# A position-bias layer computed from one constant tile of shifted log distances, half on ScalarE and half on VectorE

## The chip, the cores and the metric

The kernel runs on one core of a Trainium2 chip. The metric is the device time of one execution in microseconds (us). The kernel before was timed three times: 1243.59 us median, 1242.97 to 1249.49. A profile shows one further execution. TensorE is written PE, VectorE DVE, ScalarE ACT; SP is the queue from which all DMAs are issued.

## The reference

Attention with a learned position bias, then two gated feed-forward layers, all in fp32. The sizes are 4 batches, 8 heads, 576 positions, 64 columns per head, a hidden layer of 32 for the bias, 512 model columns, 1536 and 2048 gate columns, 2304 tokens.

```python
rel = (pos[:, None] - pos[None, :])
x = log1p(abs(rel)) / log1p(maximum(pos[:, None], 1.0))     # 576 x 576
h = maximum(x[..., None] @ w1 + b1, 0.0)                    # 32 hidden units
bias = h @ w2                                               # 8 heads
scores = q @ k.T / 8 + bias;  attn = softmax(scores);  o = attn @ v
x = (sigmoid(o @ w_gate) * (o @ w_val)) @ w_out             # first layer
h = x @ w_in;  out = (h * clip(h + 3, 0, 6) / 6) @ w_out2   # second layer
```

The numerator of x depends only on the distance between two positions, the denominator only on the row.

## The kernel before

The 576 query positions are cut into five chunks (QC): four of 128 and one of 64. For each chunk the kernel computes the bias of its rows, runs attention for its 16 units (a unit is a pair of heads of one batch; the last chunk has 8 units), and then runs the 68 weight steps of the two feed-forward layers on the chunk's 512 tokens (256 in the last).

**The bias.** Rows are taken in groups G of 16, eight groups to a chunk. The hidden layer of a group is a tile z of 128 partitions by 4 by 576: the 32 hidden units times 4 rows stand on the partitions, and the four slots g hold four rows each. Eight matmuls with w2b_t (`bias_out`, L157) turn it into 16 rows by 8 heads in PSUM; one eviction (L163 on ACT for chunk 1, L165 on DVE for the others) multiplies by 8 and a DMA stores the result to a DRAM tile, from which attention reads it per pair of heads (`bias_read`, L181).

For chunk 0 (the *lead*) x comes in as eight tiles of 288 KB (xt, L424). Matmuls with wz_t (`lead_hidden`, L121) spread x over the partitions with the weight w1 in it, ACT (L125) and DVE (L126) each take half of the result out of PSUM with bias and relu, and `lead_out` (L139) makes the output in two halves, one evicted on ACT (L144), one on DVE (L146). In the lead the order on PE, ACT, DVE and SP is the order of the program. Chunk 0's bias is stored before its first attention unit begins; two weight splits stand between.

For the other chunks x is loaded already spread over the partitions: `bias_load` (L107) brings 1152 KB per group, each row of x read 32 times, and ACT computes the relu in place in two halves of 1152 columns (L111). The tile z has three buffers.

**Attention.** `att_qk` (L212) makes scores, L227 on DVE adds the bias and takes the maximum as a minimum of negated scores, L237 on ACT the exponential, L247 on DVE the normalisation, L260 transposes on PE, L263 copies on ACT, L279 multiplies by v, and L295 and L296 split the result into two parts.

**The weights.** In the first pass over the steps (block 0) a weight tile arrives packed (L306) and `w_split` takes it apart with L321 and L331 on ACT and L322, L323, L326 and L332 on DVE; the result is also stored to DRAM (L333). Later blocks load it from there (L310). Each step is twelve matmuls (L348), and each step's evictions run on ACT and DVE (L357 and L359 make the two parts of a gate's result).

**The order of the work.** After the lead only PE's order is written by hand. Block k runs the 68 steps of chunk k; events with a due step are put between them: the bias of chunk k+1 in blocks 0 and 1 from step 2 on, one group per 1.5 steps, its matmuls in pairs of groups; the bias of chunk 3 in block 1 from step 22, one group per 5.2 steps; the bias of chunk 4 in block 2; and attention of chunk k+1 from step 21 on (from step 0.5 in blocks 2 and 3). On ACT, DVE and SP a planner orders the instructions by its own simulated times; each of these queues then runs in that order. Loads after the lead are held until the loads of the lead's last unit have been issued (`issue_after`).

Of the kernel before, what the change touches and what calls it, by code (L numbers as in the profile page):

```python
# [56 lines left out]
def fused_kernel(ctx: ExitStack, tc: tile.TileContext, qd, kd, vd, xp, xr, wz, zc, w2b, iden, wpack, out):  # L57
# [55 lines left out]
    def lead_hidden(G, j, xt):  # L113

        if j == 0:
            z_q[G] = z_p.tile([128, 4, S], F32, name="z")
        z = z_q[G]
        cs = slice(NI * j, NI * j + NI)
        ps = [s_ps(), s_ps()]
        for q in range(4):  # L120
            nc.tensor.matmul(  # L121
                out=ps[q // 2][:, q % 2, 0:NI], lhsT=wz_t[32 * q:32 * q + 32], rhs=xt[32 * q:32 * q + 32, G, cs],
                start=True, stop=True, tile_position=(32 * q, 0),
            )
        nc.scalar.activation(out=z[:, 0:2, cs], in_=ps[0][:, :, 0:NI], func=AF.Relu, bias=b1c)  # L125
        nc.vector.tensor_scalar(  # L126
            out=z[:, 2:4, cs], in0=ps[1][:, :, 0:NI], scalar1=b1c, scalar2=0.0, op0=ALU.add, op1=ALU.max
        )

    def lead_out(G, j):  # L130

        z = z_q[G]
        if j == 0:
            bo_q[G] = bo_p.tile([128, S], F32, name="bo")
        bo = bo_q[G]
        po = mm_ps()[:, 0:NI]
        cs = slice(NI * j, NI * j + NI)
        for g in range(4):
            nc.tensor.matmul(  # L139
                out=po[32 * g:32 * g + 32], lhsT=w2b_t, rhs=z[:, g, cs], start=True, stop=True,  # L140
                tile_position=(0, 32 * g),
            )
        if j == 0:
            nc.scalar.activation(out=bo[:, cs], in_=po, func=AF.Copy, scale=D ** 0.5)  # L144
        else:
            nc.vector.tensor_scalar(out=bo[:, cs], in0=po, scalar1=D ** 0.5, scalar2=None, op0=ALU.mult)  # L146
            nc.sync.dma_start(out=biasD[0][16 * G:16 * G + 16].rearrange("i h j -> (i h) j"), in_=bo)
# [390 lines left out]
def _positions():  # L538

    pos = np.arange(S)  # L540
    rel = (pos[:, None] - pos[None, :]).astype(np.float32)
    x = np.log1p(np.abs(rel)) / np.log1p(np.maximum(pos[:, None].astype(np.float32), 1.0))
    x = x.astype(np.float32)
    n = QC[0][1]
# [63 lines left out]
```

## Time and profile before

| | us |
|---|---|
| median of three runs | 1243.59 |
| profiled execution | 1242.72 |
| its span | 1240.9 |
| PE busy | 1188.8 |
| PE weight loads busy | 933.4 |
| DVE busy | 588.3 |
| ACT busy | 571.6 |
| moved by DMA | 332.43 MB |

The span is the time from the first to the last instruction of the profiled execution. A matmul in fp32 shows as two records. An engine's idle time is put down to what ended it; an engine runs its own instructions in order, so an instruction that waits holds those behind it. The clock column is the share of full speed that was granted to TensorE.

### The profile page before, as it was taken

What the parts mean: (1) busy time and instruction counts of PE and PEld (TensorE: products, weight loads), DVE (VectorE), ACT (ScalarE), POOL (GpSimd) and SP (SyncE); (2) the same over time, 40 slices, a digit from 0 to 9 for tenths busy, and PEclk for the clock granted to TensorE, in tenths of its full rate; (3) what the DMA queues carried; (4) which work ended last, traced back from release to release, by engine and by line L of the source; (5) the groups of instructions that cost most, each with busy time, mean ns of one, the idle gap of its engine ahead of it and who ended that gap; (6) DMA issues with size and microseconds to landing.
All of it is one profiled execution on the core that took longest, in us unless ns stands there. A gap on an engine that the chain in (4) does not pass through costs nothing.

```text
span 1240.9 us, 20018 instructions
## 1 busy us (share of the span) xinstructions
PE 1188.8 (96%) x7672; PEld 933.4 (75%) x7672; DVE 588.3 (47%) x1284; ACT 571.6 (46%) x1121; POOL 0.2 (0%) x4
## 2 busy tenths in 40 slices
PE   7797997999999999999999999999999999999998
PEld 3576665777778777677777777777778888788998
DVE  4786756899893333344343333253423323341232
ACT  4588775677672463455543333253412223341231
POOL 0000000000000000000000000000000000000000
PEclk9798988999999999999999999999999999999999
DMA  6779997999987896875878575767677676657997
GB/s 231 248 249 366 346 418 282 351 358 320 356 292 246 313 404 209 279 254 189 278 231 295 183 256 182 218 190 216 192 218 244 226 234 210 204 185 227 372 366 279
DMA packets 120160, 332.43 MB, mean 268 GB/s; under 512 B 20993, under 2 KB 35585, under 8 KB 116481
## 3 DMA queue, kind: packets, MB, share of 16 engines
q1 hardware_dynamic: 120064, 331.16, 78.0%
q8 instruction: 61, 1.00, 0.3%
q14 instruction: 35, 0.28, 0.1%
HBM read 280.12 MB, written 50.99 MB: 267 GB/s over the span
## 4 chain that ended last, share of the span: by engine, by line
PE 78%; DMA 8%; DVE 7%; ACT 4%; issue 2%; SPq 0%; ACTq 0%; DVEq 0%
PE ps L348 59%; PE ps L279 6%; DMA z<-xp 5%; PE ps L212 5%; PE ps L260 5%; PE ps L157 2%; DMA wd<-wpack 2%; ACT z L111 2%; PE ps L121 1%; DVE cm L323 1%; DVE wp L332 1%; DVE cm L326 1%; DVE s L227 1%; ACT s L237 1%; PE ps L139 1%
## 5 line engine op out<-in xcount | busy, mean ns | idle before, releaser
L348 PE MATMUL ps<-xyh,wp 128*128 128x512 f32 (+1 forms) x1600 | 483.8, 377 | 8.8 <-ACT pT L263 3.5
L348 PE MATMUL ps<-gh,wp 128*128 128x512 f32 (+1 forms) x1120 | 346.2, 380 | 2.8 <-DVE wp L332 1.5
L348 PEld LDWEIGHTS ps<-xyh,wp 128*128 128x128 f32 x1600 | 291.9, 190 | 73.8 <-issue 11.7
L348 PE MATMUL ps<-xyl,wp 128*128 128x512 f32 (+1 forms) x800 | 296.5, 371 | 0.7 <-DVE xyl L361 0.7
L348 PEld LDWEIGHTS ps<-gh,wp 128*128 128x128 f32 x1120 | 204.1, 189 | 46.7 <-issue 8.6
L348 PE MATMUL ps<-gl,wp 128*128 128x512 f32 (+1 forms) x560 | 207.1, 370 | 0.0
L348 PEld LDWEIGHTS ps<-xyl,wp 128*128 128x128 f32 x800 | 152.1, 190 | 23.7 <-DVE xyl L361 1.1
L263 ACT ACTIVATE pT<-ps 128x384 f32<-128x384 f32 x216 | 100.8, 487 | 116.8 <-PE ps L260 116.4
L237 ACT ACTIVATE s<-s,m 128x576 f32<-128x576 f32 x144 | 110.6, 771 | 67.1 <-DVE m L227 66.5
L357 ACT ACTIVATE gh<-tmp 128x512 fp32r<-128x512 f32 (+1 forms) x140 | 82.3, 588 | 113.0 <-DVE tmp L379 80.9
L359 DVE TENSOR_TENSOR gl<-tmp,gh 128x512 fp32r<-128x512 f32 (+1 forms) x140 | 89.3, 638 | 69.4 <-ACT gh L357 68.9
L227 DVE CUSTOM_DVE_ANT_0 s<-ps,bm 128x576 f32<-128x576 f32 x144 | 103.9, 753 | 30.0 <-PE ps L212 29.5
L348 PEld LDWEIGHTS ps<-gl,wp 128*128 128x128 f32 x560 | 106.3, 190 | 15.0
L260 PE MATMUL ps<-id_t,s 128*128 128x128 f32 x648 | 104.0, 280 | 9.9 <-DVE s L247 8.1
L260 PEld LDWEIGHTS ps<-id_t,s 128*128 128x128 f32 x648 | 80.1, 142 | 42.9 <-issue 13.2
L279 PE MATMUL ps<-pT,vt 128*64 128x128 f32 (+1 forms) x1600 | 98.3, 271 | 5.0 <-DVE xyl L296 4.4
L212 PE MATMUL ps<-kt,qt 64*128 64x288 f32 (+1 forms) x640 | 93.7, 435 | 8.0 <-DVE m L227 8.0
L279 PEld LDWEIGHTS ps<-pT,vt 128*64 128x64 f32 x1600 | 81.0, 139 | 24.8 <-issue 15.4
L379 DVE SCALAR_TENSOR_TENSOR tmp<-tmp,ps 128x512 f32<-128x512 f32 (+1 forms) x60 | 38.0, 633 | 126.4 <-PE ps L348 116.3
L111 ACT ACTIVATE z<-z,zc_t 128x1152 f32<-128x1152 f32 x56 | 72.5, 1342 | 23.8 <-DMA z<-xp 23.7
L385 DVE SCALAR_TENSOR_TENSOR tmp<-tmp,ps 128x512 f32<-128x512 f32 (+1 forms) x80 | 50.5, 631 | 66.9 <-ACT tmp L384 65.5
L296 DVE TENSOR_TENSOR xyl<-ps,xyh 128x128 fp32r<-128x128 f32 x72 | 20.8, 289 | 125.0 <-ACT xyh L295 125.0
(36 smaller groups left out, 727.8 us busy)
## 6 DMA issues: line engine op xcount, KB each, us to landing
wp<-wsp SPq DMA_DIRECT2D x272, 512.0 KB, 4.1
wd<-wpack SPq DMA_DIRECT2D x68, 512.0 KB, 5.9
wsp<-wp SPq DMA_DIRECT2D x68, 512.0 KB, 5.5
z<-xp SPq DMA_DIRECT2D x28, 1152.0 KB, 10.1
vt<-vd SPq DMA_DIRECT2D x80, 320.0 KB, 4.3
kt<-kd SPq DMA_DIRECT2D x80, 288.0 KB, 4.6
biasD<-bo SPq DMA_DIRECT2D x36, 288.0 KB, 8.4
bm<-biasD SPq DMA_DIRECT2D x16, 576.0 KB, 5.8
```

Of the source, the lines that this page charges most:

```text
L111: nc.scalar.activation(out=z, in_=z, func=AF.Relu, scale=w1c, bias=b1c)
L212: nc.tensor.matmul(out=ps[h][n * a:n * a + n, j, 0:NI], lhsT=qt[r, b + a, 0:n], rhs=kt[r, NI * j:NI * j + NI], start=True, stop=True, tile ...
L227: nc.vector.tensor_tensor_reduce(out=d["s"][:, h].rearrange("p (a j) -> p a j", a=2), in0=ps[h][:, :, 0:NI], in1=bm[:, h].rearrange("p (a ...
L237: nc.scalar.activation(out=s[:, h], in_=s[:, h], func=AF.Exp, scale=-1.0, bias=d["m"][:, h:h + 1], accum_out=r[:, h:h + 1],)
L260: nc.tensor.transpose(out=ps[:, t * NQ:t * NQ + NQ], in_=p[:, 128 * k:128 * k + 128], identity=id_t)
L263: nc.scalar.activation(out=d["pt"][:, 3 * part:3 * part + 3], in_=ps[:, 0:3 * NQ].rearrange("p (t n) -> p t n", t=3), func=AF.Copy,)
L279: nc.tensor.matmul(out=po[64 * h:64 * h + 64, n * a:n * a + n], lhsT=vt[:, v], rhs=pt[:, k, n * a:n * a + n], start=(t == 0), stop=(t == 4 ...
L348: nc.tensor.matmul(out=ps[:, 0:nt], lhsT=w[:, c, :], rhs=x[:, 0:nt], start=(first and c == 0 and i == 0), stop=(last and c == 3 and i == 2),)
L357: nc.scalar.activation(out=hi[:, 0:nt], in_=src, func=AF.Copy, scale=scale)
L359: nc.vector.tensor_tensor(out=lo[:, 0:nt], in0=src, in1=hi[:, 0:nt].bitcast(F32), op=ALU.subtract)
L379: nc.vector.scalar_tensor_tensor(out=th, in0=th, scalar=1.0, in1=ps, op0=ALU.add, op1=ALU.mult)
L385: nc.vector.scalar_tensor_tensor(out=t, in0=t, scalar=6.0, in1=ps, op0=ALU.min, op1=ALU.mult)
```

## The change

x is no longer loaded. One constant tile tz_t holds, on partition p, the numerators log1p(|distance|) for all distances, shifted by p mod 4 (1148 columns). The x of four rows is a window of 576 columns of it, at a place that depends on the rows; the reciprocal of the denominator times w1 is a scalar per partition in sc_t, one column for every four rows. For slots 0 and 1 ACT computes relu(s x + b). For slots 2 and 3 DVE computes max(s x, -b), which is smaller by b; the product of the missing b with w2, times 8, is a scalar per partition cv_t that the eviction adds. Four small DVE instructions and two small matmuls set up these scalars.

The lead uses the same functions as the other chunks: the loads of xt, the matmuls with wz_t and the evictions in halves are gone, and so are the loads into z. The upper part of tz_t is loaded first (700 of 1148 columns), the rest behind the loads of the first three units. z has two buffers in place of three. `bias_out` is cut into `bias_mm` (matmuls) and `bias_out` (eviction and store); after the lead, both groups' matmuls of a pair are issued before both evictions. The evictions use Identity with a bias in place of Copy on ACT, and a multiply and add on DVE.

```diff
-    z_p = pool("z", 3)
+    z_p = pool("z", 2)
...
+    nc.sync.dma_start(out=zc_t[:, 0:2], in_=zc)
+    nc.sync.dma_start(out=sc_t, in_=rd)
+    nc.sync.dma_start(out=tz_t[:, t0:], in_=tz[:, t0:])
     nc.sync.dma_start(out=w2b_t, in_=w2b)
+    nc.vector.tensor_scalar(out=sc_t, in0=sc_t, scalar1=zc_t[:, 0:1], scalar2=None, op0=ALU.mult)
+    nc.vector.tensor_scalar(out=zc_t[:, 2:3], in0=b1c, scalar1=-1.0, scalar2=None, op0=ALU.mult)
+    nc.vector.memset(cv_t, 0.0)
+    ps = mm_ps()
+    for g in (2, 3):
+        nc.tensor.matmul(
+            out=ps[32 * g:32 * g + 32, 0:2], lhsT=w2b_t, rhs=zc_t[:, 0:2], start=True, stop=True,
+            tile_position=(0, 32 * g),
+        )
+    nc.vector.tensor_scalar(out=cv_t[64:128], in0=ps[64:128, 1:2], scalar1=D ** 0.5, scalar2=None, op0=ALU.mult)
...
-    def bias_load(G):
-        z = z_q[G] = z_p.tile([128, 4, S], F32, name="z")
-        nc.sync.dma_start(out=z.rearrange("p g j -> p (g j)"), in_=xp[G:G + 1].broadcast_to([32, 4, 4 * S]))
-    def bias_hidden(G, g0, g1):
-        z = z_q[G][:, g0:g1]
-        nc.scalar.activation(out=z, in_=z, func=AF.Relu, scale=w1c, bias=b1c)
+    def bias_hidden(G, g):
+        if g == 0:
+            z_q[G] = z_p.tile([128, 4, S], F32, name="z")
+        t = 4 * G + g
+        z, x = z_q[G][:, g], tz_t[:, S - 4 - 4 * t:2 * S - 4 - 4 * t]
+        if g < 2:
+            nc.scalar.activation(out=z, in_=x, func=AF.Relu, scale=sc_t[:, t:t + 1], bias=b1c)
+        else:
+            nc.vector.tensor_scalar(
+                out=z, in0=x, scalar1=sc_t[:, t:t + 1], scalar2=zc_t[:, 2:3], op0=ALU.mult, op1=ALU.max
+            )
...
-            nc.scalar.activation(out=bv, in_=ps[:, :, 0:NI], func=AF.Copy, scale=D ** 0.5)
+            nc.scalar.activation(out=bv, in_=ps[:, :, 0:NI], func=AF.Identity, scale=D ** 0.5, bias=cv_t)
         else:
-            nc.vector.tensor_scalar(out=bv, in0=ps[:, :, 0:NI], scalar1=D ** 0.5, scalar2=None, op0=ALU.mult)
+            nc.vector.tensor_scalar(
+                out=bv, in0=ps[:, :, 0:NI], scalar1=D ** 0.5, scalar2=cv_t, op0=ALU.mult, op1=ALU.add
+            )
...
-        for G in range(NG0):
-            nc.sync.dma_start(out=xt[:, G], in_=xr[G])
         nc.sync.dma_start(out=id_t, in_=iden)
         for n in range(2):
             w_load(n)
         for u in us[0:3]:
             att_load(u, False)
-        for G in range(NG0 + 1):
-            for j in range(2):
-                if G < NG0:
-                    lead_hidden(G, j, xt)
-                if G:
-                    lead_out(G - 1, j)
+        nc.sync.dma_start(out=tz_t[:, 0:t0], in_=tz[:, 0:t0])
+        for G in range(QC[0][1] // 16 + 1):
+            if G < QC[0][1] // 16:
+                for g in range(4):
+                    bias_hidden(G, g)
+                bias_mm(G)
+            if G:
+                bias_out(G - 1)
...
-        ev = [(t0 - 3.0 + dt * min(g, 1), lambda G=G0 + g: bias_load(G)) for g in range(min(nG, 2))]
+        ev = []
         for g in range(nG):
-            def hidden(G=G0 + g, more=g + 2 < nG):
-                bias_hidden(G, 0, 2)
-                bias_hidden(G, 2, 4)
-                if more:
-                    bias_load(G + 2)
-            ev.append((t0 + dt * g, hidden))
+            ev.append((t0 + dt * g, lambda G=G0 + g: [bias_hidden(G, t) for t in range(4)]))
         for g in range(0, nG, 2):
             def outs(G=G0 + g):
+                for i in range(2):
+                    bias_mm(G + i)
                 for i in range(2):
                     bias_out(G + i)
```

## Rows read from the trace of the kernel before

**Rows 1.** The page: busy time, and TensorE's granted clock in 40 slices.

```profile
PE 1188.8 (96%) x7672; PEld 933.4 (75%) x7672; DVE 588.3 (47%) x1284; ACT 571.6 (46%) x1121; POOL 0.2 (0%) x4
...
PEclk9798988999999999999999999999999999999999
```

**Rows 2.** Windows: from:to, length, PE, PEld, DVE, ACT, POOL busy, clock, DMA share, GB/s.

```profile
84.70:116.40 31.70, 24.17 (x218) 18.82 (x216) 23.52 (x62) 28.99 (x61) 0.00 (x0) 0.84 0.96 363
...
131.30:171.90 40.60, 36.59 (x238) 24.72 (x237) 23.97 (x42) 30.54 (x43) 0.00 (x0) 0.92 1.01 395
...
189.90:218.00 28.10, 20.95 (x81) 15.05 (x82) 21.19 (x44) 15.83 (x28) 0.00 (x0) 0.88 0.73 264
218.00:365.00 147.00, 142.14 (x888) 110.29 (x888) 137.65 (x297) 104.50 (x217) 0.00 (x0) 1.00 0.96 344
...
500.00:568.00 68.00, 61.83 (x405) 46.56 (x404) 28.18 (x66) 35.23 (x66) 0.00 (x0) 0.97 0.76 260
568.00:672.00 104.00, 102.48 (x676) 79.20 (x675) 40.14 (x98) 49.17 (x97) 0.00 (x0) 1.00 0.78 255
```

**Rows 3.** Timeline of the first 44 us: start, length, engine, instruction, idle before.

```profile
2.11 3.76 SPq L424 DMA_DIRECT2D xt<-xr  x8
...
5.30 1.34 PE L121 MATMUL ps<-xt,wz_t 32*128 32x288 f32 x8 [5.30 <-DMA xt<-xr]
...
11.12 1.19 PE L139 MATMUL ps<-z,w2b_t 128*32 128x288 f32 x8
...
15.70 0.69 PE L139 MATMUL ps<-z,w2b_t 128*32 128x288 f32 x8
...
36.26 0.46 DVE L146 TENSOR_SCALAR bo<-ps 128x288 f32<-128x288 f32 x1 [0.49 <-ACT bo L144]
...
43.59 0.76 DVE L227 CUSTOM_DVE_ANT_0 s<-ps,bm 128x576 f32<-128x576 f32 x1 [0.38 <-DMA bm<-biasD]
```

**Rows 4.** Lines by shape: instruction, count | busy us, mean ns | idle before.

```profile
L111 ACT ACTIVATE z<-z,zc_t 128x1152 f32<-128x1152 f32 x56 | 72.5, 1342 | 23.8 <-DMA z<-xp 23.7
...
L357 ACT ACTIVATE gh<-tmp 128x512 fp32r<-128x512 f32 x112 | 70.6, 630 | 86.9 <-DVE tmp L379 62.6 <-DVE tmp L385 23.8
L247 DVE TENSOR_SCALAR s<-s,r 128x576 f32<-128x576 f32 x144 | 68.3, 516 | 2.0
...
L165 DVE TENSOR_SCALAR bo<-ps 128x576 f32<-128x576 f32 x20 | 15.0, 754 | 9.7 <-PE ps L157 9.7
L126 DVE TENSOR_SCALAR z<-ps,zc_t 128x576 f32<-128x576 f32 x16 | 13.1, 818 | 19.8 <-PE ps L121 17.0 <-issue 2.8
...
L125 ACT ACTIVATE z<-ps,zc_t 128x576 f32<-128x576 f32 x16 | 11.8, 740 | 14.4 <-PE ps L121 14.4
...
L357 ACT ACTIVATE gh<-tmp 128x256 fp32r<-128x256 f32 x28 | 11.7, 417 | 26.1 <-DVE tmp L379 18.3 <-DVE tmp L385 7.9
...
L125 ACT ACT_TABLE_LOAD x1 | 1.3, 1283 | 3.0 <-DMA zc_t<-zc 3.0
```

**Rows 5.** Timeline of ACT around L111, and PE's waits from 500 to 570.

```profile
94.44 2.59 ACT L111 ACTIVATE z<-z,zc_t 128x1152 f32<-128x1152 f32 x2 [0.50 <-DMA z<-xp]
...
106.05 2.61 ACT L111 ACTIVATE z<-z,zc_t 128x1152 f32<-128x1152 f32 x2
...
189.82 2.58 ACT L111 ACTIVATE z<-z,zc_t 128x1152 f32<-128x1152 f32 x2
...
193.06 0.66 ACT L321 ACTIVATE cm<-wd 128x512 f32<-128x512 f32 x1
...
505.39 2.59 ACT L111 ACTIVATE z<-z,zc_t 128x1152 f32<-128x1152 f32 x2 [4.40 <-DMA z<-xp]
...
L348 PE MATMUL ps<-xyh,wp 128*128 128x512 f32 x63 | 22.6, 423 | 3.5 <-ACT pT L263 3.5
```

**Rows 6.** DMA issues: KB each and median us to landing.

```profile
z<-xp SPq DMA_DIRECT2D x28, 1152.0 KB, 10.1
...
xt<-xr SPq DMA_DIRECT2D x8, 288.0 KB, 5.4
```

More of the change, by code (lines that the diff above doesn't have):

```diff
@@ L24 @@
 NF1, NF2 = DFF1 // 128, DFF2 // 128
-NG = S // 16
 QC = ((0, 128), (128, 128), (256, 128), (384, 128), (512, 64))
@@ L56, in fused_kernel @@
 @with_exitstack
-def fused_kernel(ctx: ExitStack, tc: tile.TileContext, qd, kd, vd, xp, xr, wz, zc, w2b, iden, wpack, out):
+def fused_kernel(ctx: ExitStack, tc: tile.TileContext, qd, kd, vd, tz, rd, zc, w2b, iden, wpack, out):
     nc = tc.nc
@@ L89, in fused_kernel @@
     wsp = dr_p.tile([NSTEP, 128, 2, 512], F32, name="wsp")
-    wz_t = const.tile([128, 128], F32, name="wz_t")
-    zc_t = const.tile([128, 2], F32, name="zc_t")
+    tz_t = const.tile([128, 2 * S - 4], F32, name="tz_t")
+    sc_t = const.tile([128, S // 4], F32, name="sc_t")
+    zc_t = const.tile([128, 3], F32, name="zc_t")
+    cv_t = const.tile([128, 1], F32, name="cv_t")
     w2b_t = const.tile([128, 32], F32, name="w2b_t")
     id_t = const.tile([128, 128], F32, name="id_t")
-    nc.sync.dma_start(out=wz_t, in_=wz)
@@ L96, in fused_kernel @@
-    nc.sync.dma_start(out=zc_t, in_=zc)
+    t0 = S - QC[0][1]
+    nc.sync.dma_start(out=zc_t[:, 0:2], in_=zc)
+    nc.sync.dma_start(out=sc_t, in_=rd)
+    nc.sync.dma_start(out=tz_t[:, t0:], in_=tz[:, t0:])
     nc.sync.dma_start(out=w2b_t, in_=w2b)
-    w1c, b1c = zc_t[:, 0:1], zc_t[:, 1:2]
-    z_q, bo_q = {}, {}
-    def bias_load(G):
-        z = z_q[G] = z_p.tile([128, 4, S], F32, name="z")
-        nc.sync.dma_start(out=z.rearrange("p g j -> p (g j)"), in_=xp[G:G + 1].broadcast_to([32, 4, 4 * S]))
@@ L109, in bias_hidden @@
-    def bias_hidden(G, g0, g1):
-        z = z_q[G][:, g0:g1]
-        nc.scalar.activation(out=z, in_=z, func=AF.Relu, scale=w1c, bias=b1c)
-    def lead_hidden(G, j, xt):
-        if j == 0:
-            z_q[G] = z_p.tile([128, 4, S], F32, name="z")
[L117 to L123, printed above, removed]
-            )
[L125 to L147, printed above, removed]
@@ L149, in bias_out @@
-    def bias_out(G):
+    b1c = zc_t[:, 1:2]
+    nc.vector.tensor_scalar(out=sc_t, in0=sc_t, scalar1=zc_t[:, 0:1], scalar2=None, op0=ALU.mult)
[8 more added lines that the diff above has]
+    nc.vector.tensor_scalar(out=cv_t[64:128], in0=ps[64:128, 1:2], scalar1=D ** 0.5, scalar2=None, op0=ALU.mult)
@@ L151, in bias_out, with bias_mm @@
+    def bias_mm(G):
         z = z_q.pop(G)
-        c = min(G // 8, NC - 1)
-        bo = bo_p.tile([128, S], F32, name="bo")
-        ps = s_ps()
+        ps = bo_q[G] = s_ps()
         for j in range(2):
@@ L160, in bias_out @@
                 )
+    def bias_out(G):
+        ps = bo_q.pop(G)
+        c = min(G // 8, NC - 1)
+        bo = bo_p.tile([128, S], F32, name="bo")
         bv = bo.rearrange("p (a j) -> p a j", a=2)
         if c == 1:
-            nc.scalar.activation(out=bv, in_=ps[:, :, 0:NI], func=AF.Copy, scale=D ** 0.5)
+            nc.scalar.activation(out=bv, in_=ps[:, :, 0:NI], func=AF.Identity, scale=D ** 0.5, bias=cv_t)
         else:
-            nc.vector.tensor_scalar(out=bv, in0=ps[:, :, 0:NI], scalar1=D ** 0.5, scalar2=None, op0=ALU.mult)
+            nc.vector.tensor_scalar(
+                out=bv, in0=ps[:, :, 0:NI], scalar1=D ** 0.5, scalar2=cv_t, op0=ALU.mult, op1=ALU.add
+            )
         i0 = 16 * G - QC[c][0]
@@ L416, in fused_kernel @@
     with ExitStack() as lead:
-        xl_p = lead.enter_context(tc.tile_pool(name="xl", bufs=1))
         for name, bufs in (("s", 3), ("k", 6), ("v", 7)):
@@ L538, in _positions @@
 def _positions():
[L540 to L544, printed above, removed]
-    r = np.zeros((n // 16, 4, 32, S), np.float32)
-    r[:, :, 0:4] = x[:n].reshape(n // 16, 4, 4, S)
-    xp = x.reshape(NG, 4, 4, S).transpose(0, 2, 1, 3).reshape(NG, 4, 4 * S)
-    return xp, r.reshape(n // 16, 128, S)
+    q = np.tile(np.arange(4), 32)[:, None]
+    num = np.log1p(np.abs(np.arange(2 * S - 4)[None] - (S - 4) - q).astype(np.float32))
+    den = np.log1p(np.maximum(4 * np.arange(S // 4)[None] + q, 1).astype(np.float32))
+    return num.astype(np.float32), (1.0 / den).astype(np.float32)
 def _layout(q, k, v, w1, b1, w2, moe_w_gate, moe_w_val, moe_w_out, moe2_w_in, moe2_w_out):
@@ L559, in _layout @@
     vd[:, :, :, 6:10] = vv[:, :, 1, 64:].reshape(B, HP, 4, 128, D).transpose(0, 1, 3, 2, 4)
-    wz = np.zeros((4, 32, 128), np.float32)
-    for r in range(4):
-        wz[:, r, r::4] = w1[0]
-    wz = wz.reshape(128, 128)
     zc = np.stack([np.repeat(w1[0], 4), np.repeat(b1, 4)], 1)
@@ L567, in _layout @@
         w2b[g::4, 8 * g:8 * g + 8] = w2
-    xp, xr = _positions()
+    tz, rd = _positions()
     wpack = np.empty((NSTEP, 128, 4, 128), moe_w_gate.dtype)
@@ L587, in _layout @@
             wpack[i] = blk(moe2_w_out, s[1], s[2])
-    return dict(qd=qd, kd=kd, vd=vd, xp=xp, xr=xr, wz=wz, zc=zc, w2b=w2b, iden=np.eye(128, dtype=np.float32), wpack=wpack.view(np.uint64).reshape(NSTEP, 128, 512))
+    return dict(qd=qd, kd=kd, vd=vd, tz=tz, rd=rd, zc=zc, w2b=w2b, iden=np.eye(128, dtype=np.float32), wpack=wpack.view(np.uint64).reshape(NSTEP, 128, 512))
 def kernel(**inputs):
```

2 lines of the change are left out of this document (removed).

## The prediction

> **What bounds the kernel now.** I read the page's totals first, then the windows by stage, then the first 44 us in order of time, then the lines with shapes kept apart. TensorE is busy for 1188.8 of 1240.9 us [rows 1], so at most 52 us of idle time can come back, plus what the clock takes: the granted share is 7 or 8 tenths in four of the first seven slices and 9 in all later ones. The windows say where the time is lost [rows 2]. I count a stretch's loss as its length less PE busy, plus PE busy times what is missing from a granted clock of 1.00. 84.7 to 116.4: 7.5 idle and 24.17 x 0.16 = 3.9. 131.3 to 171.9: 4.0 and 36.59 x 0.08 = 2.9. 189.9 to 218: 7.15 and 20.95 x 0.12 = 2.5. 500 to 568: 6.2 and 61.83 x 0.03 = 1.9. 568 to 672: 1.5. From 218 to 365 TensorE is 97% busy, but so are VectorE (137.65 of 147, 94%) and the DMAs (0.96): that stretch has three near-bounds. Before all this stands the lead, in which the bias of chunk 0 is finished at 36.26 + 0.46 = 36.72 us, and the first attention unit can't start before it [rows 3].
>
> **The lead.** Removed: eight 288 KB loads of xt, 128 PE records of L121, the evictions through PSUM on both engines [rows 4, 6]. Added per group: two Relus on ACT, two max instructions on DVE, all from SBUF; the output eviction is one DVE instruction of 576 instead of two halves on two engines.
> DVE: no row shows a multiply and max from SBUF. The nearest is L247, the same shape, SBUF to SBUF, scalar from a pointer, 516 ns; the upper bound is L126, two operations but out of PSUM, 818 ns [rows 4]. I take 516, for the source and the shape are L247's. The eviction is L165's shape, 754. Per group 2 x 0.516 + 0.754 = 1.79 us (upper 2.39).
> ACT: L357 at 512 and 256 columns, 630 and 417 ns, gives 0.832 ns a column; L111's 1342 ns less 576 columns is 863 for a half, two of them 1.73 per group. The lower bound is L125, 740. ACT runs beside DVE and ahead of it.
> PE: 16 records per group. L139's groups of 8 took 1.19 us at 11.12 and 0.69 at 15.70 [rows 3]: 2.38, later 1.38 or less.
> Start: tz is a 350 KB load issued about 1.6, where xt's first, 288 KB issued at 2.11, let PE start at 5.30. So it lands about 5; four small DVE instructions and two matmuls of set-up stand ahead and cost about 0.9. First group ready for PE about 7. Four groups at PE's slow 2.4 us reach 16.6, the other four go at DVE's 1.79, 23.8 with the last eviction. Gain 36.7 - 23.8 = 12.9. If PE stays slow for all eight: 7 + 19.2 + 0.75 = 27, gain 9.8; at 1.79 throughout 22, gain 15.
> What is late next: the store, the read of the bias and two weight splits; from 36.72 to the first minimum at 43.59 that is 6.9 us and is only shifted. The DMAs have room: 2.3 MB less to bring in, the same stores. The lower half of tz (229 KB) is queued on SP behind three units' loads and ahead of the stores, and is first read about 60 us later.
>
> **The hidden layer of chunks 1 to 4.** Removed: 28 loads of 1152 KB, median 10.1 us to landing [rows 6], with SP's issues, and 56 ACT instructions of 1342 ns. Added: 56 Relus of 863 and 56 DVE instructions of 516. ACT gets back 28 x (2.68 - 1.73) = 27 us, DVE pays 28.9; for the first of these chunks alone ACT 7.6, DVE 8.3.
> The added wait: z has two buffers in place of three, so a pair's hidden layer waits until PE has done the pair before. Behind it on DVE stand the weight splits (L322 to L332) and the evictions of the gates; on ACT the splits' conversions; and PE waits for the splits within two steps. Evicting after both groups' matmuls leaves PE's order as it was, and both PSUM buffers were used before.
> 84.7 to 116.4: ACT is busy 28.99 of 31.7, six L111 start there (8.1 us), the first behind a 0.50 us wait for its load [rows 2, 5]. Two buffers let only two groups in ahead of their matmuls: four halves, 3.5 us. ACT falls by 4.6 and its wait goes: I take -5. DVE rises by 2.1 to 25.6 and is next. Bounds 0 and -11.4.
> 131.3 to 171.9: the DMAs are full (1.01), ACT has 30.54 of 40.6. Without the loads what is next is DVE, 24.0 + 6 groups of 1.03 in a stretch that can't go below PE's 36.59 - 2.9 = 33.7: I take -4, bounds 0 and -6.9.
> 189.9 to 218: ACT's pair of L111 at 189.82 (2.58 us) is, by its place after the sixteen of chunk 1, work for chunk 2; a weight split's first step, L321, follows it at 193.06 [rows 5]. Lighter ACT and DMAs should leave the splits further ahead, but attention joins on DVE here: -6, bounds 0 and -9.7.
> 218 to 365: 0. DVE's load is unchanged unless hidden halves of the next chunk slip in; bounds +8.3 (16 x 0.516, all of it on a full engine) and -4.9.
> 500 to 568: ACT sat 4.40 us before the L111 at 505.39 for its load, and PE waited 3.5 us in this stretch for attention's copies, L263, which share its queue [rows 5]; no load, no such wait, and DVE is busy 28 of 68. -6.5, bounds 0 and -8.0. 568 to 672: -1, bounds 0 and -1.5.
> Identity with a bias in place of Copy for the eight evictions of chunk 1: the trace has one table load for Relu, Copy, Tanh and Exp together, 1283 ns [rows 4]. Cost 0; if Identity needed its own table, two loads for each eviction, 16 x 1.283 = 20.5 us of ACT.
>
> [...]
>
> **Sum.** 12.9 + 5 + 4 + 6 + 0 + 6.5 + 1 = 35.4 us. The profiled execution took 1242.72 us (span 1240.9 and 1.8 around it): 1207.3. The median of the three runs is 0.87 above that execution: 1208 us.
>
> **Rivals.**
> *All of it comes back.* PE is the bound up to 218, too: every low end of the terms, 15 + 11.4 + 6.9 + 9.7 + 4.9 + 8.0 + 1.5 = 57.4, 1186 us. For it: the loads and L111 end most chains there. Against: DVE and ACT each come within some per cent of PE while splits, gates and hidden halves run together.
> *VectorE eats the first block.* What ACT and the DMAs give back between 84.7 and 218 DVE takes, and its 8.3 us show in 218 to 365: -12.9 - 7.5 + 8.3 = -12.1, 1231 us. For it: DVE's 94%. Against: it has 40% free between 131.3 and 171.9, where the work falls.
> *Slower: the splits run late behind the z wait.* DVE's queue stands at a hidden half until PE frees the buffer, the split behind it comes late, PE stalls, and the clock falls, as in 189.9 to 218 now, where 18.4 us of work took 28.1: 0.53 us more for each us of work. The lead and the later blocks still give 12.9 + 7.5, and from 84.7 on nothing. If it rules 131.3 to 189.9 (50 us of work, 8 us lost now), it adds 26.5 - 8 = 18.5, so slower begins when it lasts about 4 us of work beyond; to 250 us it adds 17 more: 1242.7 + 35.5 - 20.4 + 0.9 = 1259 us. Against: the splits are planned two steps ahead and a pair has three steps' time.
> *Identity does not share the table*: at most 20.5 us on ACT between 131 and 172: 1229 us. Against: Copy and Relu share now. [...]
>
> **How the numbers follow.** Forecast 0.66, all back 0.11, VectorE 0.14, table 0.03, slower 0.06. The range 1189 to 1231 holds the forecast with its unknown terms, most of the first rival and VectorE's case; the slower case and the very bottom are outside, under 2 in 10. Within 0.5% means 1237.4 to 1249.8, what a measurement here can't tell from no change. Faster 0.91 (forecast, all back, nearly all of VectorE and the table), same 0.04, slower 0.05.
>
> **What would show it.** The last bias eviction of chunk 0 near 24 us, with PE's 16 records per group at 2.4 and then under 1.8; max instructions near 0.5 us and Relus near 0.86; one table load; no DMA named as the releaser of ACT before 120 us; PE idle under 3 us in the stretch that answers to 500 to 568; 218 to 365's answer as long as before. Wrong if the max takes 0.8, if DVE is idle before a hidden half with PE as the releaser while PE waits for a split, or if the weight steps before attention joins take over 3.5 us.

## The result, and the profile after

The changed kernel takes 1201.62 us (median of 4 runs, 1201.60 to 1201.79), the kernel before 1244.55 in 4 runs (1242.97 to 1249.49). The ratio is 0.9649, with a 95% interval of 0.9621 to 0.9677. The profiled executions are 1201.79 and 1242.72 us, spans 1200.1 and 1240.9, so the traces have 40.8 us to account for. The forecast was 1208, the range 1189 to 1231.

The page of after, which answers to [rows 1]: busy time per engine, and TensorE's granted clock in 40 slices.

```profile
PE 1163.5 (97%) x7548; PEld 922.9 (77%) x7548; DVE 612.0 (51%) x1344; ACT 543.5 (45%) x1113; POOL 0.2 (0%) x4
...
PEclk9899999999999999999999999999999999999999
```

TensorE's busy time fell by 25.3 us. Most of this is work that is gone: the lead's 128 records of L121, busy for 19.0 us in the kernel before (four records of the set-up came in, so 124 of 7672 are missing). Its line by shape (instruction, count, busy us, mean ns, idle before):

```profile
L121 PE MATMUL ps<-xt,wz_t 32*128 32x288 f32 x128 | 19.0, 543 | 7.2 <-DMA xt<-xr 5.3 <-ACT z L125 1.7
```

That leaves some 6 us for records that both kernels have. Four slices of [rows 1] stood at a clock of 7 or 8 tenths, now one does. The idle time around the busy time fell from 52.1 to 36.6.

When the time came back is read best from moments that both kernels have. Each block's pass over the 68 weight steps begins on ACT with a tanh out of a 128x512 PSUM tile. The timeline of before shows it in blocks 0, 1 and 2 (start, length, engine, instruction, idle before):

```profile
120.50 0.60 ACT L375 ACTIVATE tmp<-ps 128x512 f32<-128x512 f32 x1 [1.30 <-PE ps L348]
...
400.42 0.60 ACT L375 ACTIVATE tmp<-ps 128x512 f32<-128x512 f32 x1 [5.38 <-PE ps L348]
...
675.40 0.60 ACT L375 ACTIVATE tmp<-ps 128x512 f32<-128x512 f32 x1 [5.38 <-PE ps L348]
```

and the timeline of after:

```profile
105.19 0.60 ACT L362 ACTIVATE tmp<-ps 128x512 f32<-128x512 f32 x1 [2.01 <-PE ps L335]
...
371.38 0.60 ACT L362 ACTIVATE tmp<-ps 128x512 f32<-128x512 f32 x1 [5.38 <-PE ps L335]
...
634.47 0.60 ACT L362 ACTIVATE tmp<-ps 128x512 f32<-128x512 f32 x1 [5.38 <-PE ps L335]
```

After is 15.3 us ahead at the first, 29.0 at the second, 40.9 at the third, and nothing more comes later. With further moments from the two timelines, the whole account is:

| moment | before, us | after, us | ahead by | won in this step |
|---|---|---|---|---|
| last bias eviction of chunk 0 ends | 36.72 | 24.96 | 11.8 | 11.8 |
| first minimum of attention starts | 43.59 | 32.08 | 11.5 | -0.3 |
| first tanh of block 0 | 120.50 | 105.19 | 15.3 | 3.8 |
| last bias matmul pair of chunk 1 | 169.76 | 147.34 | 22.4 | 7.1 |
| tanh of weight step 22, block 0 | 205.53 | 177.75 | 27.8 | 5.4 |
| first tanh of block 1 | 400.42 | 371.38 | 29.0 | 1.3 |
| tanh of weight step 22, block 1 | 472.86 | 441.88 | 31.0 | 2.0 |
| first tanh of block 2 | 675.40 | 634.47 | 40.9 | 9.9 |
| end of span | 1240.9 | 1200.1 | 40.8 | -0.1 |

The windows of after, one for each line of [rows 2] in that order (from:to, length, then PE, PEld, DVE, ACT and POOL busy, granted clock, DMA share, GB/s):

```profile
73.00:101.20 28.20, 22.30 (x217) 17.62 (x217) 24.75 (x66) 21.74 (x55) 0.00 (x0) 0.94 0.89 328
...
116.00:149.50 33.50, 33.50 (x238) 23.84 (x237) 29.52 (x54) 27.75 (x45) 0.00 (x0) 1.00 0.90 309
...
149.50:180.00 30.50, 30.30 (x139) 23.91 (x139) 26.32 (x52) 19.38 (x33) 0.00 (x0) 1.00 0.90 323
180.00:340.00 160.00, 151.31 (x925) 117.01 (x923) 147.84 (x320) 110.81 (x229) 0.00 (x0) 0.99 0.93 331
...
464.00:530.00 66.00, 66.00 (x460) 50.17 (x459) 34.58 (x79) 34.17 (x71) 0.00 (x0) 1.00 0.69 218
530.00:632.00 102.00, 101.62 (x673) 78.68 (x672) 43.56 (x103) 44.72 (x95) 0.00 (x0) 1.00 0.68 211
```

The second line holds the same 238 matmul records as its line of before, in 33.5 us instead of 40.6: PE is busy all of it at a clock of 1.00, where before it had 4.0 us idle and 0.92. The stretch at 464 to 530 is full as well. Outside the lead, most of what is left is in the first window (5.9 us idle, 0.94) and in 180 to 340 (8.7 us idle, with DVE at 92% and the DMAs at 0.93).

The lead of after, from its timeline: PE's bias matmuls, the first four and the last of eight bias evictions on DVE (L150), a pair of hidden halves between two of them, hidden halves on DVE for chunk 1, and the first minimum of attention.

```profile
7.18 9.38 PE L136 MATMUL ps<-z,w2b_t 128*32 128x288 f32 x80 [1.72 <-ACT z L125]
...
10.14 0.82 DVE L150 TENSOR_SCALAR bo<-ps,cv_t 128x576 f32<-128x576 f32 x1 [2.92 <-PE ps L136]
...
11.85 0.81 DVE L150 TENSOR_SCALAR bo<-ps,cv_t 128x576 f32<-128x576 f32 x1
12.58 1.06 DVE L127 TENSOR_SCALAR z<-tz_t,sc_t,zc_t 128x576 f32<-128x576 f32 x2
13.55 0.81 DVE L150 TENSOR_SCALAR bo<-ps,cv_t 128x576 f32<-128x576 f32 x1
...
17.33 0.82 DVE L150 TENSOR_SCALAR bo<-ps,cv_t 128x576 f32<-128x576 f32 x1 [1.98 <-DMA biasD<-bo]
...
24.15 0.81 DVE L150 TENSOR_SCALAR bo<-ps,cv_t 128x576 f32<-128x576 f32 x1
...
25.21 1.07 DVE L127 TENSOR_SCALAR z<-tz_t,sc_t,zc_t 128x576 f32<-128x576 f32 x2
...
32.08 0.75 DVE L214 CUSTOM_DVE_ANT_0 s<-ps,bm 128x576 f32<-128x576 f32 x1
```

Evictions follow each other by 1.70 us with DVE never idle (11.85 to 13.55), apart from one stop of 1.98 us that ends at 17.33: the tile bo has three buffers, and the fourth eviction waits for the store of the first. That is the lead's pace: DVE's two hidden halves and one eviction per group.

The lines of after with shapes kept apart (instruction, count, busy us, mean ns, idle before), answering to [rows 4]:

```profile
L125 ACT ACTIVATE z<-tz_t,zc_t,sc_t 128x576 f32<-128x576 f32 x72 | 57.2, 858 | 5.9 <-PE ps L136 4.9 <-ACT z L125 0.8
...
L127 DVE TENSOR_SCALAR z<-tz_t,sc_t,zc_t 128x576 f32<-128x576 f32 x72 | 38.2, 575 | 1.5 <-DMA tz_t<-tz 1.5
...
L150 DVE TENSOR_SCALAR bo<-ps,cv_t 128x576 f32<-128x576 f32 x28 | 22.8, 814 | 14.0 <-PE ps L136 12.1 <-DMA biasD<-bo 2.0
...
L148 ACT ACTIVATE bo<-ps,cv_t 128x576 f32<-128x576 f32 x8 | 5.8, 728 | 0.9 <-PE ps L136 0.9
...
L125 ACT ACT_TABLE_LOAD x1 | 1.3, 1283 | 5.0 <-DMA tz_t<-tz 5.0
```

The busy time divided by the count is less than the mean (38.2 / 72 = 0.53 us against 575 ns), because each instruction starts before the one ahead of it has quite ended. In a row without a gap the pace is shorter still. In the lead an eviction holds DVE for 0.73 us (11.85 to 12.58) and two halves for 0.97 (12.58 to 13.55), from start to start; that is the 1.70 us, where twice 0.53 and an eviction's mean of 0.81 would give 1.87.

### The profile page after: what moved, and what is told of

Read it like the earlier page. It is cut to its first block, busy times and chain, and to the rows that moved or that the text cites. A ratio compares the mean times of both kernels' runs of the same rounds, so it can differ in the third digit from the quotient of the medians.

```text
span 1200.1 us, 19787 instructions
## 1 busy us (share of the span) xinstructions
PE 1163.5 (97%) x7548; PEld 922.9 (77%) x7548; DVE 612.0 (51%) x1344; ACT 543.5 (45%) x1113; POOL 0.2 (0%) x4
## 4 chain that ended last, share of the span: by engine, by line
PE 79%; DVE 9%; DMA 7%; ACT 2%; issue 2%; SPq 0%; DVEq 0%; ACTq 0%
PE ps L335 61%; PE ps L266 6%; PE ps L199 5%; PE ps L247 5%; DMA wd<-wpack 5%; PE ps L136 2%; DVE cm L310 2%; DVE cm L313 1%; DVE s L214 1%; DVE wp L319 1%; ACT cm L308 1%; DMA wsp<-wp 1%; DVE gl L346 1%; DVE cm L309 1%; ACT wp L318 0%
## 5 line engine op out<-in xcount | busy, mean ns | idle before, releaser
L224 ACT ACTIVATE s<-s,m 128x576 f32<-128x576 f32 x144 | 110.6, 771 | 73.4 <-DVE m L214 73.1
L247 PE MATMUL ps<-id_t,s 128*128 128x128 f32 x648 | 103.1, 279 | 13.0 <-DVE s L234 11.4
L247 PEld LDWEIGHTS ps<-id_t,s 128*128 128x128 f32 x648 | 79.8, 142 | 45.5 <-issue 9.9
L199 PEld LDWEIGHTS ps<-kt,qt 64*128 64x128 f32 (+1 forms) x640 | 51.2, 178 | 30.9 <-DVE m L214 9.8
```

What stands on the lines that cost most here:

```text
L199: nc.tensor.matmul(out=ps[h][n * a:n * a + n, j, 0:NI], lhsT=qt[r, b + a, 0:n], rhs=kt[r, NI * j:NI * j + NI], start=True, stop=True, tile ...
L224: nc.scalar.activation(out=s[:, h], in_=s[:, h], func=AF.Exp, scale=-1.0, bias=d["m"][:, h:h + 1], accum_out=r[:, h:h + 1],)
L247: nc.tensor.transpose(out=ps[:, t * NQ:t * NQ + NQ], in_=p[:, 128 * k:128 * k + 128], identity=id_t)
```

## The experiments

Three explanations compete for the 41 us: the work in the lead (no matmuls and evictions for the first layer, half of the hidden layer on DVE), the 28 loads of 1152 KB that no longer cross the DMAs, and the removal of ACT's work and of ACT's waits for these loads in chunks 1 to 4. Each kernel is read by four lengths of its own profile: the end of the last bias eviction of chunk 0, the first tanh of block 0 (T0), and the lengths of blocks 0 and 1 between first tanhs. From the first tanh of block 2 to the end of the span every kernel but e3 (575.2) took 565.5 to 566.1 us.

| kernel | time, us | last eviction | T0 | block 0 | block 1 |
|---|---|---|---|---|---|
| before | 1242.72 | 36.72 | 120.50 | 279.92 | 274.98 |
| after | 1201.79 | 24.96 | 105.19 | 266.19 | 263.09 |
| e1, lead alone | 1232.66 | 23.43 | 107.31 | 283.97 | 274.13 |
| e2, all halves on ACT | 1223.55 | 32.66 | 115.13 | 274.18 | 266.93 |
| e3, loads as well | 1249.96 | 23.69 | 102.26 | 279.74 | 290.89 |
| e4, loads' traffic to nowhere | 1281.25 | 25.14 | 103.04 | 347.43 | 263.07 |
| e5, that traffic paced | 1210.91 | 25.21 | 102.85 | 276.99 | 263.09 |
| e6, all halves on DVE | 1205.18 | 29.02 | 109.95 | 264.84 | 263.09 |
| e7, fourth weight buffer | 1195.67 | 24.75 | 105.03 | 259.90 | 263.07 |
| e8, six bo buffers in the lead | 1202.62 | 22.76 | 103.83 | 268.39 | 263.08 |
| e9, e7 and weights preloaded | 1195.12 | 28.41 | 108.58 | 256.11 | 263.09 |
| e10, e7, e8 and e9 | 1191.28 | 23.00 | 103.29 | 257.59 | 263.09 |

Two parts of the change have no run of their own: z's third buffer, and the order of a pair's matmuls and evictions. The planner also orders each kernel anew, so a run differs from after by more than its edit. How much that can be shows in T0: e3, e4 and e5, which only add loads or traffic, reach it 2.1 to 2.9 us before after does, and why is not shown.

Times are of the profiled execution. The kernel before took 1248.92 us beside e1 to e4 and 1248.52 beside e5 to e8, one run each.

**e1: only the lead is new.** Chunks 1 to 4 go back to loads and a Relu in place on ACT with three z buffers; chunk 0 stays new.

```diff
+    def bias_load(G):
+        z = z_q[G] = z_p.tile([128, 4, S], F32, name="z")
+        nc.sync.dma_start(out=z..., in_=xp[G:G + 1].broadcast_to([32, 4, 4 * S]))
-            ev.append((t0 + dt * g, lambda G=G0 + g: [bias_hidden(G, t) for t in range(4)]))
...
+            ev.append((t0 + dt * g, hidden))
```

Here `hidden` is the Relu in place on ACT and then `bias_load(G + 2)`; `z...` and `...` stand for what is left out.

> Only the lead is new; chunks 1 to 4 load x into three z buffers and compute the relu on ACT in place, as before. If the lead's 11.8 us (last bias eviction 36.7 to 25.0) is a gain of its own and the other 29 us belong to the later chunks: about 1232 us, the first pair of bias matmuls of chunk 1 about 11 to 12 us earlier than before (131.3 to about 119.7) and not 15.3, and everything later by the same 11 to 12 us. Rival, the lead's gain is eaten by a load or a weight split that is late next: 1238 us or more, the first pair less than 8 us earlier.

Measured: 1232.66 us. T0 from its timeline, with the starts of blocks 1 and 2:

```profile
107.31 0.60 ACT L370 ACTIVATE tmp<-ps 128x512 f32<-128x512 f32 x1 [1.77 <-PE ps L343]
...
391.28 0.60 ACT L370 ACTIVATE tmp<-ps 128x512 f32<-128x512 f32 x1 [5.38 <-PE ps L343]
...
665.41 0.60 ACT L370 ACTIVATE tmp<-ps 128x512 f32<-128x512 f32 x1 [5.38 <-PE ps L343]
```

It is 13.2 us ahead of before at T0, gives 4.1 back in block 0 (283.97 against 279.92), and ends 10.1 ahead of the profiled before (16.3 ahead of the single run beside it, which is at the top of what the kernel before takes; so the lengths inside the profiles are what I go by). The lead is a quarter of the 40.8; three quarters are in chunks 1 to 4.

**e2: all hidden halves on ACT.** No DVE max anywhere, so no missing b to add back either; no loads.

```diff
-        if g < 2:
+        if True:
```

> All four slots of the hidden layer on ACT from the constant tile, none on DVE; no x is loaded. ACT's work per group is 4 x 0.86 = 3.4 us, above the 2.68 of the kernel before. Theory that the loads (landing and the waits on them) cost the blocks their 29 us: the gain behind the lead mostly stays; the lead becomes ACT's, 8 x 3.2 us, 8 to 11 us longer than with both engines, and the total is about 1212 us. Rival, that moving half of the layer from ACT to DVE is what freed the blocks: the gain behind the lead goes too, 1230 us or more.

Measured: 1223.55, between the two expectations and 21.8 us above after: 9.9 by T0, 8.0 in block 0, 3.8 in block 1. The lead now has ACT's pace, as DVE's last eviction waits for PE, and PE for ACT, in every group (timeline, 3.03 us from eviction to eviction):

```profile
28.81 0.82 DVE L148 TENSOR_SCALAR bo<-ps,cv_t 128x576 f32<-128x576 f32 x1 [2.21 <-PE ps L134]
31.84 0.82 DVE L148 TENSOR_SCALAR bo<-ps,cv_t 128x576 f32<-128x576 f32 x1 [2.21 <-PE ps L134]
```

What it decides is block 1. Here ACT carries 4 x 0.86 = 3.4 us per group, more than the 2.68 of the kernel before, and still block 1 is 8.1 us shorter than before (266.93 against 274.98). So of the 11.9 us won in block 1, at most 3.8, the difference between e2 and after, is ACT's lighter work; 8 or more came with the loads, by their traffic or by the waits for them.

**e3: the loads come back, into z.** The new hidden layer stays; each z buffer is first filled by the old load, whose data is then overwritten and not used.

```diff
-        if g == 0:
+        if G < 8 and g == 0:
             z_q[G] = z_p.tile([128, 4, S], F32, name="z")
```

> The kernel after, with the 28 loads of 1152 KB put back into z at their old due steps; the hidden layer of chunks 1 to 4 is then written over them, so it waits for them as before but costs ACT and DVE what it costs now (two z buffers). Theory of the loads: about 1225 us, with DMA z named as ACT's releaser again and idle PE in the first two blocks. Rival, the halves on two engines: 1201 to 1206 us.

Measured: 1249.96 us, all of the gain lost, where 1225 was expected. Both engines stand in order behind a load. The waits of e3 (engine and line, what it waited for: total us, times, longest):

```profile
DVE z L131 <- DMA z<-xp: 53.4, 16, 7.6
...
ACT z L129 <- DMA z<-xp: 42.6, 17, 9.2
```

and the one of this kind that the kernel before has:

```profile
ACT z L111 <- DMA z<-xp: 23.7, 15, 4.4
```

Block 1 is 27.8 us longer than after's, block 0 13.6. This is the wait and the traffic together, and with two z buffers in place of before's three it is larger than what the change removed; it shows that such waits reach the end of a block, not how much they cost before.

**e4: the traffic without the wait.** The same 28 transfers at the same planned places, but into scratch memory that nobody reads.

```diff
+    zz = [dr_p.tile([32, 4, 4 * S], F32, name=f"zz{i}") for i in range(8)]
+    def bias_load(G):
+        nc.sync.dma_start(out=zz[G % 8], in_=xp[G:G + 1].broadcast_to([32, 4, 4 * S]))
```

> The kernel after, with 28 transfers of the same 1152 KB (read from the same source, written to a scratch tensor in DRAM) at the loads' old due steps; nothing waits for them. If bandwidth and the queue behind the loads were the cost: 1215 us or more, with the packed weights landing later. If the in-order wait for the landing was the cost: 1201 to 1206 us. The difference between this run and the one with loads into z is the wait.

Measured: 1281.25 us. It was not the test it was meant to be: with nobody waiting, all 28 were issued between 75 and 195 us, eight of them ahead of T0 and twenty in block 0. Block 0 grew by 81.2 us (347.43 against 266.19), T0 fell by 2.1, so block 0 ended 79.1 us later; block 1 didn't change. The issues of e4 (count, KB each, median us to landing) and the longest piece of its chain of waits from 120 to 215 us:

```profile
zz<-xp SPq DMA_DIRECT2D x28, 1152.0 KB, 18.5
```

```profile
129.65 21.68 DMA wd<-wpack
```

A packed weight wd took up to 21.7 us to land, and PE waits for the split that follows it: its weight loads waited for the split's step on ACT (L323) 61.7 us in all, 12 times, the longest 14.7. This is what extra traffic does in block 0: 79.1 / 28 = 2.8 us per transfer when they come in a bunch.

**e5: the traffic paced.** As e4, but each transfer is issued behind the latest weight load.

```diff
     def bias_load(G):
+        with tc.issue_after(issued["w"].ins):
```

> The kernel after with the 28 transfers that nothing waits for, as in the run with traffic alone, but each put behind the weight load of its due step, so that eight fall into the first block and the others into the blocks where they were before the change. In the run without this all 28 fell into the first block and cost 79 us there, 2.8 us each. If bandwidth is the bound of the first block alone: 8 x 2.8 = 23 us there and nothing in the later blocks (first weight step of the second block 22 to 25 us later than in the kernel after, and the same distance at the end), 1224 us. If bandwidth hurts in every block: 1240 us or more. If only the wait cost anything: under 1206 us.

Measured: 1210.91, under the 1224 of the first branch and above the 1206 of the last. Eight transfers, the number of groups of chunk 1, are issued between 74 and 128 us: five ahead of T0, where the kernel before had three of these loads, and three behind it. The next three come at the very end of block 0. Block 0 takes 276.99 us, 10.8 longer than after's; as T0 is 2.3 earlier, it ends 8.5 later. In block 1 the transfers cost nothing. In block 0 PE's matmuls wait for splits, on ACT and on DVE, which the same list of after does not have (total us, times, longest):

```profile
PE ps L341 <- ACT wp L324: 7.7, 3, 3.7
...
PE ps L341 <- DVE wp L325: 2.6, 2, 1.7
```

Issues of e5, and its windows 105 to 145 and 379.8 to 450.3 (columns as above):

```profile
zz<-xp SPq DMA_DIRECT2D x28, 1152.0 KB, 8.5
```

```profile
105.00:145.00 40.00, 36.29 (x223) 26.05 (x222) 30.76 (x54) 27.48 (x44) 0.00 (x0) 0.98 0.92 368
...
379.80:450.30 70.50, 70.50 (x402) 53.64 (x401) 31.63 (x54) 27.53 (x42) 0.00 (x0) 1.00 0.96 369
```

The answering windows of after; in each kernel the second line begins at its first tanh of block 1:

```profile
105.00:145.00 40.00, 40.00 (x244) 29.99 (x243) 34.12 (x62) 32.02 (x51) 0.00 (x0) 1.00 0.80 274
...
371.40:441.90 70.50, 70.50 (x402) 53.66 (x401) 31.60 (x54) 27.54 (x43) 0.00 (x0) 1.00 0.70 224
```

In block 0 the DMAs moved 368 instead of 274 GB/s, and PE lost 3.7 of 40 us. In block 1 they moved 369 instead of 224, a share of 0.96 instead of 0.70, and PE did the same 402 records in the same 70.50 us. So in block 0 the traffic alone gives back 8.5 to 10.8 of the 13.7 us won there, by whether the earlier T0 is counted, and in block 1 none of the 11.9. A reserve: e5's transfers write to memory and not to SBUF, and no run compares the two.

**e6: all hidden halves on DVE.** This loads the engine that the forecast feared for.

```diff
-        if g < 2:
+        if False:
```

> All four slots of the hidden layer on DVE, none on ACT. Theory that DVE is near its bound in the lead (it sets the 1.7 us per group) and in the first block (94% busy from 218 to 365 before): lead 7 us longer, first block 6 to 10 longer, about 1216 us. Rival, DVE has room behind the lead: 1209 us. In either case the later blocks are as in the kernel after.

Measured: 1205.18, 3.4 us above after, less than either branch expected. It comes from the lead: the last eviction is 4.1 later, T0 4.8, block 0 is 1.3 shorter, block 1 equal. Last eviction, and the hidden halves among the lines of e6:

```profile
28.20 0.82 DVE L150 TENSOR_SCALAR bo<-ps,cv_t 128x576 f32<-128x576 f32 x1
```

```profile
L127 DVE TENSOR_SCALAR z<-tz_t,sc_t,zc_t 128x576 f32<-128x576 f32 x144 | 73.7, 576 | 1.7 <-DMA tz_t<-tz 1.4 <-PE ps L136 0.2
```

DVE took 35.5 us more work and no block grew. Its 92% between 180 and 340 is not a bound on the hidden layer, which falls elsewhere.

**e7: a fourth buffer for the packed weights.** After's own chain of waits has the packed weight load in it; of the three lines here the first two stand ahead of T0, the third in block 0:

```profile
73.89 6.60 DMA wd<-wpack
...
82.76 7.34 DMA wd<-wpack
...
160.51 9.02 DMA wd<-wpack
```

```diff
-    wf_p = pool("wf", 3)
+    wf_p = pool("wf", 4)
```

> A fourth buffer for the packed weights. The chain of waits of the kernel after holds the load of packed weights for 5% of the span, most of it in the first block. If that wait is a matter of buffers: 1192 to 1198 us. If the first block is held by the DMAs' bandwidth and by DVE: 1200 to 1203 us.

Measured: 1195.67; block 0 is 6.3 us shorter, and nothing else changed. So part of what bounds block 0 of after is how early its packed weights are asked for.

**e8: six bo buffers for the lead.** This takes away the store that DVE waits for at 17.33.

```diff
-        bo = bo_p.tile([128, S], F32, name="bo")
+        bo = (A["bo"] if c == 0 else bo_p).tile([128, S], F32, name="bo")
+        A["bo"] = lead.enter_context(tc.tile_pool(name="bol", bufs=6))
```

> Six output buffers in the lead in place of three. In the kernel after one eviction of the lead waited 1.98 us for the store three before it. If that is on the path: the last eviction of chunk 0 at about 23.0 in place of 24.96 and 1199.6 us. If another wait takes its place: 1201 us or more.

Measured: 1202.62, no gain in one run. The last eviction ends at 22.76, 2.2 us earlier, with its start in the timeline at

```profile
21.94 0.82 DVE L150 TENSOR_SCALAR bo<-ps,cv_t 128x576 f32<-128x576 f32 x1
```

T0 is only 1.4 earlier, and block 0 is 2.2 longer. So what bounds block 0 did not move with the lead's end; that it is the packed weights again fits e7 and e10, but this run alone doesn't show it.

**e9: e7, and all first weights loaded in the lead.**

```diff
-        for n in range(2):
+        for n in range(WA):
             w_load(n)
-    for n in range(2, WA):
-        w_load(n)
```

> Four packed-weight buffers, and the first four packed weights loaded at the start of the lead in place of two (the third and fourth then wait for nothing at the lead's end). In the kernel after two weight loads of 6.6 and 7.3 us stand on the chain between 73.9 and 90.2. If they held the end of the lead: 2 to 4 us below the run with four buffers alone (1195.7), 1192 to 1194 us. If ACT and DVE hold it: 1195 to 1196 us.

Measured: 1194.9 (4 runs, 1194.35 to 1196.58); ratio to before 0.9599 (0.9579 to 0.9619). The preloads stand ahead of the bias stores, and the fourth eviction waits longer for its buffer:

```profile
19.95 0.82 DVE L150 TENSOR_SCALAR bo<-ps,cv_t 128x576 f32<-128x576 f32 x1 [4.33 <-DMA biasD<-bo]
```

So the lead ends 3.4 us later, and block 0 takes 10.1 less than after's, 3.8 less than e7's. From last eviction to T0 it is 80.2 us as in after (80.2), and from the first minimum of attention 72.3 against 73.1: the two wd loads that were moved held at most 0.8 us of it.

**e10: e7, e8 and e9 together.** With six bo buffers the preloads cost the lead 0.2 us (last eviction at 23.00, in e8 at 22.76).

> The three edits together: four packed-weight buffers, four packed weights loaded in the lead, six output buffers in the lead. The output buffers gave the lead 2.2 us that the first block took back, where it was bound by the weights' loads; with a fourth buffer that bound is looser. If so the 1.3 to 2.2 us stay: 1190 to 1194 us. If the first block takes them back again: 1193 to 1196 us.

Measured: 1190.2 us (4 runs, 1189.64 to 1191.28) against 1245.7 of before (7 runs, 1242.27 to 1248.03); ratio 0.9558 (0.9535 to 0.9580). It beats both kernels, after by 11 us. Its page, and the shares of its chain:

```profile
PE 1162.3 (98%) x7548; PEld 923.0 (78%) x7548; DVE 611.7 (51%) x1344; ACT 544.4 (46%) x1113; POOL 0.2 (0%) x4
```

```profile
PE 92%; DVE 5%; DMA 1%; issue 1%; ACT 0%; SPq 0%; DVEq 0%; ACTq 0%
```

against the chain of after:

```profile
PE 79%; DVE 9%; DMA 7%; ACT 2%; issue 2%; SPq 0%; DVEq 0%; ACTq 0%
```

The DMAs' share of the chain went from 7% to 1%, and PE is idle for 27 us of the span.

## Why the prediction was right, point by point

The direction and the three places (lead, first block, block 1) were right, and the sum was 35.4 us where the profiled executions differ by 40.9. The terms:

| step | forecast | measured |
|---|---|---|
| lead, to the last eviction | 12.9 | 11.8 |
| to the first tanh (84.7 to 116.4) | 5 | 3.5 |
| chunk 1's bias (131.3 to 171.9) | 4 | 7.1 |
| 189.9 to 218 | 6 | 5.4 |
| 218 to 365 | 0 | 1.3 |
| start of block 1 (400 to 473) | not priced | 2.0 |
| 500 to 568 and 568 to 672 | 7.5 | 9.9 |

**The lead.** The end was predicted at 23.8 and came at 24.96, and that it was so near is partly luck: both paces were taken too slow, and a stall was left out that nearly made up for it. DVE's pace is 1.70 per group, not 1.79: the mean lengths are longer than taken (575 and 814 ns instead of 516 and 754), but the instructions overlap at their ends, and the pace goes from start to start. PE did not set the pace of the first four groups at 2.4: five groups took 9.38 us, 1.88 each, and it waits for hidden halves, so DVE sets the pace from the first eviction on. From 10.14, where the first starts, 7 x 1.70 and 0.82 give 22.9, and the last one ended at 24.96: what is missing is the stop of 1.98 us for the store of bo, which the prediction did not name; with six buffers (e8) it was 22.76. e2 and e6 show the same rule with other engines: 3.03 us per group where ACT has all four halves, 2.68 where DVE has them.

**What comes after it.** The next term came 1.5 us short of its -5, though no hidden work at all is left on ACT between 73 and 101 us. DVE is next there, as the prediction said: it is busy 24.75 of the 28.20 us, and the largest wait of TensorE's matmuls in this stretch of after is for attention's scaling on DVE (total us, times, longest):

```profile
PE ps L247 <- DVE s L234: 5.0, 3, 3.1
```

TensorE's weight loads waited longer, 6.5 us, for the exponential on ACT (L224) that stands ahead of this scaling, so DVE is not alone there. The landings of wd that the chain shows here hold little of it: e9 loads two weights earlier and is 0.8 us faster from attention's first minimum on. Nor does the loads' traffic hold it: from the first minimum of attention to T0 after takes 73.1 us, e4 and e5 with traffic 70.8 and 70.5, e1 with the Relu in place back on ACT 77.1, the kernel before 76.9. That points to L111 and its waits on ACT, as the prediction had it. One sign was wrong: ACT does wait for DMAs before 120 us, not for z but for tz_t at the start (5.0 us) and for wd.

**Chunk 1's bias is the term that was mis-sized**, 7.1 instead of 4. The bounds were 0 and -6.9, and it came out at the low end or just beyond it: PE is busy 33.50 of 33.50 at a clock of 1.00. I had stopped at 4 for DVE as the next bound. It isn't: DVE is busy 29.52 of the 33.50 while PE never stands, and in e6 with twice the hidden work block 0 was no longer. Here an engine that was busy 88% and worked ahead of PE cost PE nothing. Block 0 in three pieces, from the timelines, in us (T0 to the last bias matmul pair of chunk 1, from there to weight step 22, from there to block 1):

| kernel | to the last pair | to step 22 | to block 1 |
|---|---|---|---|
| before | 49.26 | 35.77 | 194.89 |
| after | 42.15 | 30.41 | 193.63 |
| e1, lead alone | 51.49 | 34.45 | 198.03 |
| e2, all halves on ACT | 42.15 | 37.31 | 194.72 |
| e5, traffic paced | 47.95 | 34.87 | 194.17 |
| e6, all halves on DVE | 42.15 | 29.46 | 193.23 |
| e7, fourth weight buffer | 42.16 | 29.35 | 188.39 |

The first piece is this term. It is the same with all halves on either engine, so neither engine's work bounds it; the traffic alone gives back 5.8 of the 7.1 us. The prediction put the gain to ACT and the loads together, and here it was the loads. The second piece is the term of 6: traffic gives back 4.5 of its 5.4, but all halves on ACT give back 6.9. There the two causes overlap and can't be told apart by adding.

**Block 1.** 9.9 instead of 7.5, and 2.0 before it that had no term. The stretch that answers to 500 to 568 has no idle PE time, as "what would show it" asked. The mechanism, no load and so no wait on ACT's queue ahead of attention's copies, fits: traffic cost nothing in e5, ACT's work explains at most 3.8 (e2), and waits for loads reach the block's end (e3, 27.8 us longer). The first 2.0 us stay whole in e2 and in e5. The kernel before's own chain of waits from 473 to 680 us has the load in it: PE's matmuls free a buffer of z, the load follows 0.05 us later, and L111 waits for its landing.

```profile
495.06 1.15 PE ps L157 x16
...
496.26 9.10 DMA z<-xp
...
505.39 2.59 ACT z L111 x2
```

The chain has two more such loads, at 543.11 and 641.70. So the cause is shown by elimination and by this chain; the one run that would have isolated it, loads into three buffers beside the new hidden layer, was not made.

**The rivals.** VectorE does not eat the first block: in e6, with all halves on it, block 0 took 264.84 us, in after 266.19. The slower case does not happen: DVE is never idle before a hidden half with PE as the releaser while PE waits for a split, since PE is full from 116 to 149.5, where the two buffers are used; up to step 22 of block 0 a weight step took 3.30 us on average (72.56 / 22), under the 3.5 of the third sign. All of it came back only between 116 and 149.5 and at the end of block 1; 180 to 340 kept 8.7 us idle, and the term of 0 for 218 to 365 holds: from step 22 of block 0 to block 1 it is 194.9 us before and 193.6 after. Its reason, three near-bounds, is not the whole of it: with one more weight buffer (e7) the same stretch took 188.4. Identity needed no table of its own: one load of 1283 ns in the whole trace of after, with Identity, Relu, Copy, Tanh and Exp.

**The price of a half on ACT.** It was taken as 863 ns from rows, whose instruction carried two pointers as this one does, and measured 858.

## What to carry to other kernels

Where data can be computed from a small constant tile on engines with room, take the load away and look for the gain in two places: in a stretch where the DMAs are full (here at a share of 1.01), other landings get earlier (a packed weight's longest fell from 13.5 us to 9.1); in a stretch where they are not (0.76 from 500 to 568), what was won came, by elimination, from the wait at the head of an in-order engine's queue: of block 1's 11.9 us e5's traffic took back none, and all halves on ACT 3.8. Price a fast loop by the distance from one start to the next, not by mean length (in the lead 1.70 us per group, where the means of two halves and an eviction add up to 1.96), and look at which store or load frees each of its buffers. Once the work goes faster, ask what lands too late next: here a fourth weight buffer, six eviction buffers and earlier first loads gave another 11 us.
